# Six places for raw blocks in the y phases, and four small moves around them

## The chip, the cores and the metric

The kernel runs on one core of a Trainium2 chip. A core has five engines that run side by side, each with its own queue of instructions: PE (matrix products, 128 x 128 weights against up to 512 columns), DVE (vector work), ACT (copies and activations), POOL (here only small powers and products) and SP (here only the issue of transfers between the device memory and the on-chip memory). Engines wait for one another by semaphores. The metric is the device time of one execution in microseconds (us).

## The reference

Two kinds of layers are applied in turn, each twice, to a 2048 x 512 matrix `x`, all in float32:

```python
def _A_ref(x, dft_seq_re, dft_seq_im, dft_hid_re, dft_hid_im):
    a = jnp.einsum("bsd,ed->bse", x, dft_hid_re)
    b = jnp.einsum("bsd,ed->bse", x, dft_hid_im)
    y = jnp.einsum("ts,bse->bte", dft_seq_re, a) - jnp.einsum("ts,bse->bte", dft_seq_im, b)
    return y

def _B_ref(x, w1, w2, w3, w4):
    h = _gelu(_layernorm(x, axis=-1) @ w1)
    # the four quarters of h are shifted by +1, -1, +2, -2 rows
    hs = jnp.concatenate([g0, g1, g2, g3], axis=-1) @ w2
    x1 = x + hs
    h2 = _gelu(_layernorm(x1, axis=-1) @ w3) @ w4
    return x1 + h2

x = x + _A_ref(_layernorm(x, axis=-1), ...)
x = x + _B_ref(_layernorm(x, axis=-1), B_w1, B_w2, B_w3, B_w4)
x = x + _A_ref(_layernorm(x, axis=-1), ...)
x = x + _B_ref(_layernorm(x, axis=-1), B_w1, B_w2, B_w3, B_w4)
```

## The kernel before, in words

**Products.** Each float32 operand is split into a high part (rounded to the type `fp32r`) and a low part (the rest). A product is three matmuls (`mm3`, lines 282 to 284): high by high, high by low, low by high. So every block that comes from memory goes through ACT (the high part, a cast) and DVE (the low part, a subtraction) before PE may use it.

**Layer A.** The 2048 rows of the result are made in four chunks `c` of 512. The sequence transform is done with the block tricks of a fast matrix product, so that a chunk has two phases of eight steps `k`: an x phase (`x_phase`, products of sums of the input blocks in `ax`) and a y phase (`y_phase`, products of the blocks in `ay`). The hook of an x phase counts half steps, `i` from 0 to 15. Chunk 0 of the first layer is done without these sums (`plain_phase`), while the input is normed for the first time. A y phase has for each `k` two items, `by1` and `by0`, of 12 matmuls each, 192 in all. An item's block is the difference of two blocks of the transform matrix: DVE makes the difference (line 234, `ring..f<-raw,raw`), ACT its high part (line 235), DVE its low part (line 245). The hidden transform of chunk `c` (`hid`, tiles `rr`) runs inside the x phase of chunk `c + 1`; that of the last chunk runs behind the last y phase.

**The queue of blocks.** `pieces` lists all blocks in the order of their loading, 512 KB each, `items` the split blocks in the order of their use. A raw block lands in one of four places (`raw_at`, piece `i` in place `i % 4`), is split into one of four slots of `ring`, and PE reads the slots. `issue_dma` writes the next load into SP's program as soon as all items that use the place's old block stand in the program. SP issues in that order, and an issue waits until the old block has in fact been read. SP's one queue also carries the stores and loads of the rows of the result (`rows`: `x1d`, `xs`, `tmp`) and the shuffles `zd`, `zt`. The program keeps eight completion counters in turn, so that a transfer's issue also waits for the transfer eight ahead of it.

**Around the last y phase of a layer.** The result of a chunk is added to the input (`add_y`) in two halves of two tiles, followed by their row statistics (`y_stats`: DVE, then two operations of POOL) and a store to `x1d`. For chunk 2 the first half comes in the x phase of chunk 3, and the statistics of the second half (tiles 10 and 11) run at `k == 2` of the y phase of chunk 3 (`late["y"]`). In the same stretch the first four tiles are prepared for layer B: they are loaded back into `xs` (`BACK`), normed on ACT (line 330; tiles 0 and 1 at half step 12 of the x phase, 2 and 3 at half step 15), transposed by four DVE operations at `k == 0` of the y phase (line 594, `turned`), stored in shuffled order (`zd`, four transfers) and loaded again (`zt`).

**Layer B.** Behind the last hidden transform comes the mix (`by_pairs`): 32 slots, `shifted` (product with `w1`, gelu, shift) and `mixed` (product with `w2`), four of each for a chunk. The lists `D(slot, ...)` and `A(slot, ...)` hang other work on slots: `D` ahead of the slot's own DVE or ACT work, `A` behind it. Then the pairs of chunks go through the two large products; the last pair ends the program.

**The head.** Before the first matmul the first tile of the input is summed up by `stats` (DVE and POOL), DVE writes the first normed quarter blocks (`part_highs`, line 327), ACT the high part of the first half block (line 1465), DVE its low part (`block_low`, line 1468). The first matmuls stand in line 414: four of high by high, four of high by low, four of low by high, and again for the second pair of banks.

Of the kernel before, what the change touches and what calls it, by code (L numbers as in the profile page):

```python
# [43 lines left out]
def spectral_mlp_kernel(ctx: ExitStack, tc: tile.TileContext, x, ws, hs, w1, w2, w34, out):  # L44
# [58 lines left out]
    rg = [[at(f"rg{i}{g}", RR + (4 * i + g) * 2 * CH, 2, CH) for g in range(KD)] for i in range(2)]  # L103
    ring, ringf = zip(*(both(f"ring{i}", RNG + i * 4 * CH, 2, 2, CH) for i in range(RING)))
    raw_at = [at(f"raw{i}", RAWS + i * 2 * CH, 2, CH, dtype=F32) for i in range(RAW)]

    blk, blkf = {}, {}
    for i, word in (("11", H3), ("21", H3 + 4 * CH), ("12", RNG), ("22", RNG + 4 * CH)):
# [34 lines left out]
        return tmps[(count["tmp"] - 1) % len(tmps)]  # L143


    pieces, items, w_items, w_pieces = [], [], [], []

    def piece(src, a=0, b=2):
        pieces.append((src, a, b))
# [10 lines left out]
    for layer in range(LAYERS):  # L160
        for c in range(NC):
            if layer == 0 and c == 0:
                for k in range(NP):
                    item("plain", piece(ws[c, k][:, 2:4]))
                    item("plain", piece(ws[c, k][:, 0:2]))
                continue
            for k in range(NP):
                if c:
                    for h in range(NP):
                        if HAT[h] == k:  # L170
                            item("plain", piece(hs[HORDER[h % 4]]))
                p = piece(ws[c, k][:, 2:4])
                item("plain", p)
                item("one", p, span=(0, 1))
            ps = [(piece(ws[c, k][:, 2:4]), piece(ws[c, k][:, 0:2])) for k in range(NP)]
            for k, kind in y_order():
                item(kind, *ps[k])
        for o in HORDER:
            item("plain", piece(hs[o]))
        w_items.append(len(items))  # L180
        for i in range(2):
            item("plain", piece(w1[i]), dest=w12[i])
        for i in range(2):
            item("plain", piece(w2[i]), dest=w12[2 + i])
        w_pieces.append(len(pieces))
# [5 lines left out]
    state = {"dma": 0, "one": 0, "two": 0, "use": 0, "made": 0, "done": 0, "limit": 0, "load": w_pieces[0]}  # L191
    x_left = [(0, 1), (1, 1)] + [(j, 2) for j in range(2, NT, 2)]

    def load_x():
# [8 lines left out]
    def issue_dma(upto=None):  # L203
        while state["dma"] < (state["load"] if upto is None else upto):
            i = state["dma"]
            if i >= RAW and any(n >= state[stage] for n, stage in uses[i - RAW]):
                break
            src, a, b = pieces[i]
            raws[i] = raw_at[i % RAW]
            nc.sync.dma_start(raws[i][:, a:b], src)  # L210
            state["dma"] += 1
            if i % 2 and i > 3:
                load_x()
# [261 lines left out]
    def x_phase(c, hook):  # L475
        h = 0
        for k in range(NP):
            first, last = k == 0, k == NP - 1
            while c and h < NP and HAT[h] == k:
                s = stream()  # L480
                ri, dp = HORDER[h % 4]
                hid(ri, dp, s, PD, 2 * (h // 4), h % 4 == 0, h % 4 == 3)
                if h % 4 == 3:
                    add_y(c - 1, h // 4, PD, X1, 2 * k if h < 4 else "y")
                h += 1
            s = stream()
            run_late(2 * k)
# [75 lines left out]

    ln1, ln2 = {}, {}

    def add_y(c, half, ps, to, defer=None):
        j = c * TC + 2 * half
        for i in range(2):
            add(to[:, i], ps[i], to[:, i])
        if defer is None:  # L570
            y_stats(j, to)
        else:
            late.setdefault(defer, []).append(lambda: y_stats(j, to))

    def y_stats(j, to):
        for known, mrs in zip((ln1, ln2), stats_twice([to[:, 0], to[:, 1]])):
# [137 lines left out]
    def by_pairs(layer, zs, xin, dst):  # L714
# [17 lines left out]
        def A(slot, *fs):  # L732
            todo.setdefault((slot, 1), []).extend(fs)
# [115 lines left out]
        A(4, z_highs(1))  # L849
        D(5, z_lows(1))  # L850

        A(1, back(10, x1d), norm(8, 9))
        D(2, turn(sc0, 2, 0))
        D(3, turn(sc0, 2, 1))
        A(5, norm(10, 11))
# [588 lines left out]
    for layer in range(LAYERS):  # L1444
# [4 lines left out]
        for c in range(NC):  # L1449
            if layer == 0 and c == 0:  # L1450
                raws[0] = raw_at[0]
                for i in (1, 0):
                    load_x()
                    nc.sync.dma_start(raws[0][:, i], pieces[0][0][:, i])
# [35 lines left out]

                xp[0] = stats([xt(0)])
                block_high(1)
                block_low(1)
                part_highs(0)
                normed_act(pairs[0][:, 0], xt(0), xp[0][0])
                block_high(0)
                xp[0] += stats([xt(1)])
# [41 lines left out]
            def hook(i):  # L1539
                k, odd = divmod(i, 2)  # L1540
                if layer == 0 and c == 1:
# [4 lines left out]
                    if i == 3:  # L1546
                        xp_lows(NP - 1, False)
                    w4_split(2 * NP + i)
                if c == 0:
                    if layer:  # L1550
                        for step, f in zip((0, 0, 1), (ay_sums, ay_highs, ay_lows)):
# [29 lines left out]
            def hook(k):  # L1581
# [15 lines left out]

        tmps[:] = singles
        count["tmp"] = 0
# [2 lines left out]
        for i, (ri, dp) in enumerate(HORDER):  # L1602
# [76 lines left out]
```

## Time and profile before

| | |
|---|---|
| median of 3 runs | 1429.75 us (1428.42 to 1429.76) |
| the profiled execution | 1429.24 us, its span 1427.3 us |
| PE busy | 1420.0 us, 6261 instructions |
| DVE busy | 1168.8 us |
| ACT busy | 732.1 us |
| POOL busy | 79.7 us |
| transfers | 307.57 MB, 215 GB/s over the span |

The span goes from the first instruction's start to the last one's end. Matmuls overlap, so the busy time of PE says nothing of small gaps: those are read from the distance between the starts of matmuls. "idle before" is the time that an engine stood still ahead of an instruction, and behind `<-` stands what ended it. An SP row tells when a transfer was issued; where rows are merged (`x4`), the time is that of all of them.

### The profile page before, as it was taken

How to read it: one execution, taken by the hardware profiler on the slowest of the kernel's cores; microseconds unless marked ns; L12 is line 12 of the kernel's file. 1: busy time of each engine (PE TensorE's matmuls, PEld its weight loads, DVE VectorE, ACT ScalarE, POOL GpSimd, SP SyncE). 2: the span in 40 equal slices, each digit the busy share in tenths (PEclk: the TensorE clock that was granted, in tenths of full speed). 3: DMA queues.
4: the chain of work that ended last, by engine and by line, in shares of the span. 5: the costliest groups of instructions: out<-in, count | busy, mean ns of one | idle time of the engine just before them, and what ended most of it. 6: DMA issues, size and time to landing. Idle time of an engine off the chain costs nothing.

```text
span 1427.3 us, 17317 instructions
## 1 busy us (share of the span) xinstructions
PE 1420.0 (99%) x6261; PEld 1173.8 (82%) x6261; DVE 1168.8 (82%) x1642; ACT 732.1 (51%) x992; POOL 79.7 (6%) x105
## 2 busy tenths in 40 slices
PE   9999999999999999999999999999999999999998
PEld 7888888888888888888888888888877888888887
DVE  7986998988979888666799989889889787656676
ACT  5663464455565754434455644544555665433351
POOL 2100000000002000000000000000000020000000
PEclk9999999999999999999999999999999999999999
DMA  7866656657754857944645566575777458477764
GB/s 253 278 207 206 206 191 223 212 175 270 270 163 121 290 199 253 362 159 164 223 160 191 182 231 211 175 244 184 232 250 240 139 156 309 159 243 282 241 206 159
DMA packets 127828, 307.57 MB, mean 215 GB/s; under 512 B 9216, under 2 KB 50176, under 8 KB 124544
## 3 DMA queue, kind: packets, MB, share of 16 engines
q1 hardware_dynamic: 127744, 306.48, 64.2%
q8 instruction: 49, 0.80, 0.2%
q14 instruction: 35, 0.29, 0.1%
HBM read 252.18 MB, written 54.26 MB: 215 GB/s over the span
## 4 chain that ended last, share of the span: by engine, by line
PE 96%; DVE 2%; DMA 2%; issue 0%; SPq 0%; ACT 0%; DVEq 0%
PE psd L283 10%; PE psd L282 10%; PE psd L284 10%; PE psa L283 8%; PE psa L282 8%; PE psa L284 8%; PE psc L283 7%; PE psc L284 7%; PE psc L282 7%; PE psb L283 7%; PE psb L282 7%; PE psb L284 7%; DMA raw<-in_ws 2%; DVE ring L245 1%; DVE ring2f L234 0%
## 5 line engine op out<-in xcount | busy, mean ns | idle before, releaser
L228 ACT CAST ring<-raw 128x1024 fp32r<-128x1024 f32 x127 | 132.9, 1052 | 80.3 <-PE psd L284 41.1
L245 DVE TENSOR_TENSOR ring<-raw,ring 128x1024 fp32r<-128x1024 f32 x126 | 153.4, 1219 | 12.8 <-ACT ring L228 12.6
L282 PE MATMUL psd<-ring,rr 128*128 128x512 f32 x208 | 80.9, 389 | 0.0
L283 PE MATMUL psd<-ring,rr 128*128 128x512 f32 x208 | 80.9, 389 | 0.0
L284 PE MATMUL psd<-ring,rr 128*128 128x512 f32 x208 | 80.9, 389 | 0.0
L322 POOL TENSOR_TENSOR rs<-ve,mhalf 128x4 f32<-128x4 f32 x16 | 28.7, 1796 | 609.6 <-DVE nm L321 609.6
L301 POOL TENSOR_TENSOR rs<-ve,mhalf 128x2 f32<-128x2 f32 (+2 forms) x33 | 28.8, 872 | 547.5 <-DVE nb L300 528.6
L235 ACT CAST ring<-ring0f 128x1024 fp32r<-128x1024 f32 x28 | 29.5, 1054 | 57.7 <-DVE ring0f L234 57.7
L619 ACT ACTIVATE tmp<-rest 128x512 f32<-128x512 f32 x30 | 19.0, 632 | 73.2 <-DVE rest L468 72.8
L245 DVE TENSOR_TENSOR ring<-ring1f,ring 128x512 fp32r<-128x512 f32 (+1 forms) x56 | 53.2, 950 | 0.7 <-ACT ring L231 0.7
L330 ACT ACTIVATE tmp<-xs,nb,rs 128x512 f32<-128x512 f32 x56 | 43.2, 808 | 14.4 <-POOL nb L302 13.1
L283 PE MATMUL psb<-ring,ay 128*128 128x512 f32 x128 | 50.2, 392 | 0.4 <-DVE ring L245 0.4
L283 PE MATMUL psc<-ring,ay 128*128 128x512 f32 x128 | 49.9, 390 | 0.3 <-DVE ring L245 0.3
L282 PE MATMUL psb<-ring,ay 128*128 128x512 f32 x128 | 49.8, 389 | 0.0
L284 PE MATMUL psb<-ring,ay 128*128 128x512 f32 x128 | 49.8, 389 | 0.0
L284 PE MATMUL psc<-ring,ay 128*128 128x512 f32 x128 | 49.8, 389 | 0.0
L282 PE MATMUL psc<-ring,ay 128*128 128x512 f32 x128 | 49.8, 389 | 0.0
L235 ACT CAST ring<-ring1f 128x1024 fp32r<-128x1024 f32 x28 | 29.5, 1054 | 39.2 <-DVE ring1f L234 39.2
L282 PE MATMUL psa<-ring,ay 128*128 128x512 f32 x126 | 49.2, 390 | 0.3 <-ACT rr00f L501 0.3
L283 PE MATMUL psa<-ring,ay 128*128 128x512 f32 x126 | 49.1, 389 | 0.0
L282 PE MATMUL psd<-ring,ay 128*128 128x512 f32 x126 | 49.0, 389 | 0.0
L283 PE MATMUL psd<-ring,ay 128*128 128x512 f32 x126 | 49.0, 389 | 0.0
(657 smaller groups left out, 4439.9 us busy)
## 6 DMA issues: line engine op xcount, KB each, us to landing
raw<-in_ws SPq DMA_DIRECT2D x183, 512.0 KB, 5.0
w4r<-w4d SPq DMA_DIRECT2D x66, 512.0 KB, 4.4
raw<-in_hs SPq DMA_DIRECT2D x56, 512.0 KB, 3.6
w3b<-w3d SPq DMA_DIRECT2D x14, 1792.0 KB, 7.9
w3d<-w3b SPq DMA_DIRECT2D x5, 1792.0 KB, 6.9
x1d<-tmp SPq DMA_DIRECT2D x12, 512.0 KB, 6.2
xs<-x1d SPq DMA_DIRECT2D x12, 512.0 KB, 5.2
w4d<-w4in SPq DMA_DIRECT2D x11, 512.0 KB, 5.0
```

The source lines that it names most:

```text
L228: nc.scalar.copy(dest[:, a:b, 0], r[0][:, a:b])
L235: nc.scalar.copy(dest[:, :, 0], lo)
L245: nc.vector.tensor_tensor(lo, src, hi.bitcast(F32), op=ALU.subtract)
L282: nc.tensor.matmul(o, lh, rh, start=first, stop=False, skip_group_check=more)
L283: nc.tensor.matmul(o, lh, rl, start=False, stop=False, skip_group_check=more)
L284: nc.tensor.matmul(o, ll, rh, start=False, stop=last, skip_group_check=more)
L301: nc.gpsimd.tensor_tensor(rs[:, :n], ve[:, :n], mhalf[:, 0, :n], op=ALU.pow)
L322: nc.gpsimd.tensor_tensor(rs, ve, mhalf[:, :, :2], op=ALU.pow)
L330: nc.scalar.activation(o, s, AF.Identity, bias=mr[2], scale=mr[1])
L619: nc.scalar.activation(g_of, ps_of, AF.Gelu_apprx_tanh)
```

## The change

Five edits, all in the order of work; no arithmetic is changed.

1. Two more places for raw blocks are laid over parts of the on-chip memory that are free in the y phases (one over a buffer of the `w4` weights' preparation). They are open from half step 11 of an x phase to the end of the y phase behind it (`state["wide"]`), for the blocks of y phases alone. A load now takes the free place whose block is oldest, not place `i % 4`. This holds for all seven y phases.
2. In the y phase of chunk 3 the norms of tiles 2 and 3 move from half step 15 of the x phase to `k == 0` of the y phase, and the four transposes are split: two at `k == 0`, two at `k == 1`.
3. The statistics of tiles 10 and 11 leave this y phase: they run in slot 2 of the mix, on the copy of the rows that is loaded into `xs[5]`.
4. That load moves ahead, from slot 1 of the mix into the hidden transform ahead of it.
5. In the head, `part_highs(0)` stands ahead of `block_low(1)`.

The names behind an underscore in the rows below are buffer numbers; `raw4` and `raw5` are the new places, and line numbers of the changed program are up to 11 higher.

DVE at the start of the program, before and then changed: `rr00` and `ay0` are the first normed quarter blocks, `ring0<-raw0` is the low part of the first half block.

```order
L299 TENSOR_SCALAR ve_294<-mv_290 128x1
L300 TENSOR_SCALAR nb_292<-mv_290 128x1
L1468 TENSOR_TENSOR ring0_176<-raw0_184,ring0_176 128x512
L327 TENSOR_SCALAR rr00_160<-xs0_149,mv_290,rs_291 128x256
L327 TENSOR_SCALAR ay0_108<-xs0_149,mv_290,rs_291 128x256
L296 BN_STATS st_310<-xs0_149 128x6
```

```order
L310 TENSOR_SCALAR ve_296<-mv_292 128x1
L311 TENSOR_SCALAR nb_294<-mv_292 128x1
L338 TENSOR_SCALAR rr00_160<-xs0_149,mv_292,rs_293 128x256
L338 TENSOR_SCALAR ay0_108<-xs0_149,mv_292,rs_293 128x256
L1479 TENSOR_TENSOR ring0_176<-raw0_184,ring0_176 128x512
L307 BN_STATS st_312<-xs0_149 128x6
```

The two normed blocks pass the low part; what follows is the same.

DVE in the y phase of chunk 3 of the second layer, before and then changed, from the items of `k == 1` on (`ring..f<-raw,raw` is the difference for one item, `ring<-ring..f` the low part of the item ahead):

```order
L245 TENSOR_TENSOR ring2_180<-ring2f_181,ring2_180 128x2x512
L594 STREAM_TRANSPOSE turned0_157<-tmp_68 128x16x32 x4
L234 TENSOR_TENSOR ring0f_177<-raw1_185,raw0_184 128x2x512
L245 TENSOR_TENSOR ring3_182<-ring3f_183,ring3_182 128x2x512
...
L245 TENSOR_TENSOR ring2_180<-ring2f_181,ring2_180 128x2x512
L316 BN_STATS st_7614<-tmp_68 128x6 x2
L318 BN_AGGR mv_7611<-st_7614 128x2 x2
L319 TENSOR_SCALAR ve_7615<-mv_7611 128x2
L320 TENSOR_SCALAR ve_7615<-mv_7611 128x2
L321 TENSOR_SCALAR nm_7616<-mv_7611 128x2
L234 TENSOR_TENSOR ring0f_177<-raw1_185,raw0_184 128x2x512
```

```order
L256 TENSOR_TENSOR ring2_180<-ring2f_181,ring2_180 128x2x512
L603 STREAM_TRANSPOSE turned0_157<-tmp_68 128x16x32 x2
L245 TENSOR_TENSOR ring0f_177<-raw0_184,raw3_187 128x2x512
L256 TENSOR_TENSOR ring3_182<-ring3f_183,ring3_182 128x2x512
L245 TENSOR_TENSOR ring1f_179<-raw0_184,raw3_187 128x2x512
L256 TENSOR_TENSOR ring0_176<-ring0f_177,ring0_176 128x2x512
L603 STREAM_TRANSPOSE turned0_157<-tmp_68 128x16x32 x2
L245 TENSOR_TENSOR ring2f_181<-raw2_186,raw1_185 128x2x512
```

Two transposes stand one pair of items later, and the seven instructions of the statistics are gone from this place.

SP in the same stretch, before and then changed: `raw<-in_ws` loads a block, `x1d` takes finished rows, `zd1` the transposed tiles.

```order
L201 DMA xs1_150<-x1d_76 128x2x512
L210 DMA raw2_186<-in_ws 128x1024
L210 DMA raw3_187<-in_ws 128x1024
L201 DMA xs2_151<-x1d_76 128x2x512
...
L201 DMA x1d_76<-tmp_68 128x2x512
L210 DMA raw2_186<-in_ws 128x1024
L210 DMA raw3_187<-in_ws 128x1024
L604 DMA zd1_78<-turned0_157 32x16x128 x4
L210 DMA raw0_184<-in_ws 128x1024
L210 DMA raw1_185<-in_ws 128x1024
```

```order
L204 DMA xs1_150<-x1d_76 128x2x512
L221 DMA raw5_189<-in_ws 128x1024
L221 DMA raw4_188<-in_ws 128x1024
L221 DMA raw3_187<-in_ws 128x1024
L221 DMA raw0_184<-in_ws 128x1024
L204 DMA xs2_151<-x1d_76 128x2x512
...
L221 DMA raw2_186<-in_ws 128x1024
L613 DMA zd1_78<-turned0_157 32x16x128 x4
L221 DMA raw5_189<-in_ws 128x1024
L221 DMA raw4_188<-in_ws 128x1024
```

One pair of loads more stands ahead of `xs2` and ahead of the four `zd1` stores; behind those only one pair of y blocks is left, where there were two.

The diff, without the unchanged lines:

```diff
@@ places and state
+    raw_at += [at(f"raw{RAW + i}", word, 2, CH, dtype=F32) for i, word in enumerate((EXT + 4 * D, STG))]
...
+            y_pieces.update(i for p in ps for i in p)
...
+    held = {i: None for i in range(len(raw_at))}
@@ def issue_dma(upto=None):
             i = state["dma"]
-            if i >= RAW and any(n >= state[stage] for n, stage in uses[i - RAW]):
+            free = [
+                r
+                for r, p in held.items()
+                if (r < RAW or state["wide"] and i in y_pieces)
+                and (p is None or all(n < state[stage] for n, stage in uses[p]))
+            ]
+            if not free:
                 break
             src, a, b = pieces[i]
-            raws[i] = raw_at[i % RAW]
+            r = min(free, key=lambda r: (-1 if held[r] is None else held[r], r))
+            held[r] = i
+            raws[i] = raw_at[r]
@@ def x_phase(c, hook):
-                    add_y(c - 1, h // 4, PD, X1, 2 * k if h < 4 else "y")
+                    at_mix = c == NC - 1 and h > 4
+                    add_y(c - 1, h // 4, PD, X1, "10" if at_mix else 2 * k if h < 4 else "y", xs[5] if at_mix else X1)
@@ def add_y
-        late.setdefault(defer, []).append(lambda: y_stats(j, to))
+        late.setdefault(defer, []).append(lambda: y_stats(j, to if kept is None else kept))
@@ def by_pairs
-        A(1, back(10, x1d), norm(8, 9))
+        A(1, norm(8, 9))
+        D(2, lambda: run_late("10"))
         D(2, turn(sc0, 2, 0))
@@ the head
                 block_high(1)
+                part_highs(0)
                 block_low(1)
-                part_highs(0)
@@ x phase, hook
+                if i == 11:
+                    state["wide"] = True
...
-                if c == NC - 1 and i in (12, 15):
-                    for j in (0, 1) if i == 12 else (2, 3):
+                if c == NC - 1 and i == 12:
+                    for j in (0, 1):
                         normed_act(tmp[:, j], xt(j), ln2[j])
@@ y phase, hook
-                if c == NC - 1 and k == 0:
-                    for q in range(TC):
+                if c == NC - 1 and k < 2:
+                    for q in (2 * k, 2 * k + 1):
                         turn_one(turned0, q, tmp[:, q])
+                    for j in (2, 3)[: 2 - 2 * k]:
+                        normed_act(tmp[:, j], xt(j), ln2[j])
...
             y_phase(c, hook)
+            state["wide"] = False
@@ the last hidden transform
-            if i < 2:
-                j = (6, 8)[i]
+            if i < 3:
+                j = (6, 8, 10)[i]
                 rows(xs[j // 2], x1d, j, 2, True)
```

More of the change, by code (lines that the diff above doesn't have):

```diff
@@ L143, in tmp_tile @@
         return tmps[(count["tmp"] - 1) % len(tmps)]
-    pieces, items, w_items, w_pieces = [], [], [], []
+    pieces, items, w_items, w_pieces, y_pieces = [], [], [], [], set()
     def piece(src, a=0, b=2):
@@ L190, in spectral_mlp_kernel @@
     raws, slots, sums = {}, {}, {}
-    state = {"dma": 0, "one": 0, "two": 0, "use": 0, "made": 0, "done": 0, "limit": 0, "load": w_pieces[0]}
+    held = {i: None for i in range(len(raw_at))}
+    state = {"wide": False, "dma": 0, "one": 0, "two": 0, "use": 0, "made": 0, "done": 0, "limit": 0, "load": w_pieces[0]}
     x_left = [(0, 1), (1, 1)] + [(j, 2) for j in range(2, NT, 2)]
@@ L564, in spectral_mlp_kernel, with add_y @@
     ln1, ln2 = {}, {}
-    def add_y(c, half, ps, to, defer=None):
+    def add_y(c, half, ps, to, defer, kept=None):
         j = c * TC + 2 * half
@@ L569, in add_y @@
             add(to[:, i], ps[i], to[:, i])
-        if defer is None:
-            y_stats(j, to)
-        else:
-            late.setdefault(defer, []).append(lambda: y_stats(j, to))
+        late.setdefault(defer, []).append(lambda: y_stats(j, to if kept is None else kept))
     def y_stats(j, to):
@@ L1451, in spectral_mlp_kernel @@
                 raws[0] = raw_at[0]
+                held[0] = 0
                 for i in (1, 0):
```

## The prediction

> **What bounds the kernel.** I read the head of the page first, then who PE waited for, then the starts of its matmuls phase by phase, and at the one phase that is too long the chain of work and the rows of the other engines.
>
> ```profile
> span 1427.3 us, 17317 instructions
> PE 1420.0 (99%) x6261; PEld 1173.8 (82%) x6261; DVE 1168.8 (82%) x1642; ACT 732.1 (51%) x992; POOL 79.7 (6%) x105
> ```
>
> ```profile
> PE psd L137 <- POOL mhalf L56: 1.4, 1, 1.4
> PE psb L414 <- DVE rr L327: 1.1, 1, 1.1
> PE psb L283 <- DVE ring L245: 0.4, 1, 0.4
> PE psc L283 <- DVE ring L245: 0.3, 1, 0.3
> PE psa L282 <- ACT rr00f L501: 0.3, 1, 0.3
> ```
>
> PE is the bound. Its waits (total us, times, longest) are 1.1 at the first real matmul and three short ones. The view of stretches (start:end, length, then the busy time of PE, PEld, DVE, ACT, POOL, the granted clock, the DMA share) gives three y phases, cut at the starts of their first matmul and of the next phase's first one: chunk 3 of the first layer, chunk 2 and chunk 3 of the second.
>
> ```profile
> 344.17:387.85 43.68, 43.68 (x194) 35.96 (x192) 42.62 (x47) 22.43 (x26) 2.23 (x2) 1.00 0.73 248
> 951.51:995.03 43.52, 43.52 (x193) 36.04 (x192) 40.31 (x43) 20.99 (x25) 2.23 (x2) 1.00 0.60 200
> 1049.43:1095.21 45.78, 44.73 (x194) 35.68 (x193) 43.52 (x47) 22.39 (x26) 2.24 (x2) 1.00 0.71 233
> ```
>
> A y phase has 192 matmuls. The middle one takes 43.52, so one matmul per 0.2267 us at a granted clock of 1.00. Chunk 3 takes 0.16 more in the first layer and 2.26 more in the second. With 1.1 at the head, that is about all a reordering can win: 3.5 us of 1429, or 0.25%. Anything beyond must come as a loss.
>
> The Trainium skill ("TensorE: Matmul & The Clock Gate", "Wait — 56ns, not 53.3ns?") puts warm matmuls at N / 2.4 GHz + about 2.5 ns from start to start, an estimate of 215.8 ns for 512 columns and 41.4 us for this phase; by it the long phase would hold 4.4 us and the sum below would be 2.1 larger. The three rows here agree on 226.7 at different DMA shares, and I go by them.
>
> **Edits 2 and 3, the last y phase of a layer.** First what stops PE there. Of ACT, DVE and PE in the second layer:
>
> ```profile
> 1051.94 1.52 ACT L330 ACTIVATE tmp<-xs,nb,rs 128x512 f32<-128x512 f32 x2
> 1053.36 1.04 ACT L501 COPY rr00f<-psa 128x512 f32<-128x512 f32 x2
> ```
>
> ```profile
> 1054.22 2.49 DVE L594 STREAM_TRANSPOSE turned<-tmp 128x512 f32<-128x512 f32 x4
> 1056.62 1.19 DVE L234 TENSOR_TENSOR ring0f<-raw,raw 128x1024 f32<-128x1024 f32 x1
> 1057.72 1.22 DVE L245 TENSOR_TENSOR ring<-ring3f,ring 128x1024 fp32r<-128x1024 f32 x1
> ```
>
> ```profile
> 1061.63 0.39 PE L282 MATMUL psc<-ring,ay 128*128 128x512 f32 x1
> ```
>
> The two norms (1.52) stand on ACT ahead of the drain of `psa`, which PE waits for; the four transposes (2.49) hold the low part of `ring3` until 1058.94. Item `by1` of `k` = 2, the fifth, starts at 1061.63; without stops it would at 1049.43 + 4 x 12 x 0.2267 = 1060.31. So 1.32 of the 2.26 is lost by then, the other 0.94 later.
>
> With the norms behind the drain, `psa` is free 1.5 earlier, against a wait of 0.3. The norms then stand ahead of the cast of `ring0`, whose source DVE writes no earlier than now; that is their cover, and if it went they would cost their 1.52 less the slack of a ring slot. With two transposes instead of four DVE reaches the low part of `ring3` 1.2 earlier, at 1057.7, and PE needs it one matmul into the fourth item, 1049.43 + 3 x 2.72 + 0.23 = 1057.8. So this is just enough even if no block lands earlier; the later two transposes have DVE's lead behind them, 2.72 - 2.2 (two operations, 1.1 from start to start) = 0.5 per item.
>
> The statistics cost DVE the distance between two rows:
>
> ```profile
> 1065.67 1.28 DVE L316 BATCH_NORM_STATS2 st<-tmp 128x6 f32<-128x512 f32 x2
> 1067.42 1.23 DVE L234 TENSOR_TENSOR ring0f<-raw,raw 128x1024 f32<-128x1024 f32 x1
> ```
>
> 1.75 us. DVE is then left with 43.52 - 1.75 = 41.8 of work in a phase of 43.52. The first layer's phase shows that it can do 42.62 in 43.68 with PE losing 0.16, so 41.8 fits. In the mix the same 1.75 lands in slot 2, in front of a transpose:
>
> ```profile
> 1124.65 0.71 DVE L594 STREAM_TRANSPOSE scr<-extra 128x512 f32<-128x512 f32 x1
> 1126.65 0.69 DVE L659 TENSOR_TENSOR rg<-gt,rg 128x512 fp32r<-128x512 f32 x1 [1.29 <-ACT rg L658]
> ```
>
> ```profile
> 1127.88 0.39 PE L282 MATMUL psd<-w,rg 128*128 128x512 f32 x1
> 1129.69 0.39 PE L284 MATMUL psd<-w,rg 128*128 128x512 f32 x1
> ```
>
> DVE idles 1.29 between these two rows, so the low part of `rg` ends 0.5 later, near 1127.8; PE reads it in the ninth matmul of the slot, at 1129.69. Cost nothing, with 1.9 of cover in each layer. POOL's power and product follow the statistics to where POOL is idle; the norm that needs them hangs on slot 5, three slots on. The load of `xs[5]` (edit 4) only moves ahead, behind the weights; nothing there waits for it.
>
> **Edit 1, the places.** The later 0.94 is late blocks. From the chain of work (start, us), from DVE, and from SP:
>
> ```profile
> 1043.93 5.62 DMA raw<-in_ws
> ...
> 1065.03 7.81 DMA raw<-in_ws
> ...
> 1076.86 5.02 DMA raw<-in_ws
> ```
>
> ```profile
> 1082.01 1.22 DVE L234 TENSOR_TENSOR ring1f<-raw,raw 128x1024 f32<-128x1024 f32 x1 [1.00 <-DMA raw<-in_ws]
> ```
>
> ```profile
> 1065.49 5.34 SPq L604 DMA_DIRECT2D zd<-turned  x4
> 1070.95 6.34 SPq L210 DMA_DIRECT2D raw<-in_ws  x4
> ```
>
> A block takes 5 to 8 us from issue to landing, and with four places a pair is asked for only when the pair two ahead has been read: two pairs are 2 x 24 x 0.2267 = 10.9 us of PE, less DVE's own lead. With six there are 16.3. The blocks that arrive last (landed near 1076.86 + 5.02 = 1081.9) were asked for behind four `zd` stores that held SP 5.34. In the new order one pair more stands ahead of these stores, and the last pair may be issued some 5 us later than it must. A raw load moved past `x1d` delays that store by two issues; its buffer is overwritten at the phase's end, far behind. So I take all 0.94. In the other five y phases nothing waits now (the 43.52 row is one of them), so the places can only cost there: two more loads in flight, nothing as long as no other transfer is needed sooner. For the extra traffic the trace has no row; the bounds are nothing and, if each of the seven phases lost what the busier first-layer phase loses, 7 x 0.16 = 1.1; I take nothing, since that loss has the four transposes beside it. A gain there is excluded by 43.52 being PE's own pace.
>
> The DMA page of the Trainium skill ("DMA: Bandwidth & Descriptors", "Queues, rings and completion order") says that each DMA engine takes descriptors in ring order, so transfers behind the extra raw blocks wait for them. The long landings above agree; by this rule alone `zd` would land later by two blocks, and it is a reason for the third rival below.
>
> **Edit 5, the head.**
>
> ```profile
> 4.98 0.62 ACT L1465 CAST ring<-raw 128x512 fp32r<-128x512 f32 x1 [2.75 <-DMA raw<-in_ws]
> ```
>
> ```profile
> 8.05 0.73 POOL L301 TENSOR_TENSOR rs<-ve,mhalf 128x1 f32<-128x1 f32 x1 [2.59 <-DVE nb L300]
> ```
>
> ```profile
> 5.63 0.69 DVE L1468 TENSOR_TENSOR ring<-raw,ring 128x512 fp32r<-128x512 f32 x1 [1.08 <-ACT ring L1465]
> 6.24 0.41 DVE L327 TENSOR_SCALAR rr<-xs,mv,rs 128x256 fp32r<-128x256 f32 x1
> ...
> 7.96 0.41 DVE L1489 TENSOR_TENSOR rr<-tmp,rr 128x256 fp32r<-128x256 f32 x1
> ...
> 8.83 0.41 DVE L327 TENSOR_SCALAR rr<-xs,mv,rs 128x256 fp32r<-128x256 f32 x1
> ```
>
> ```profile
> 6.79 0.70 PE L414 MATMUL psb<-ring,rr 128*128 128x512 f32 x2 [1.05 <-DVE rr L327]
> ...
> 8.71 0.61 PE L414 MATMUL psb<-ring,rr 128*128 128x512 f32 x2
> ```
>
> DVE stands still until 5.63 for ACT's cast. The normed blocks need only POOL's power, which for this tile took 0.56:
>
> ```profile
> 4.64 0.56 POOL L301 TENSOR_TENSOR rs<-ve,mhalf 128x1 f32<-128x1 f32 x1 [3.28 <-DVE nb L300]
> ```
>
> It ends at 5.20; at the second tile DVE started 0.05 behind the power (8.05 + 0.73 to 8.83), so `rr` runs from 5.25 to 5.66 and the first matmul, 0.14 behind it as now (6.65 to 6.79), starts at 5.80: 0.99 sooner. But DVE's chain begins only 5.63 - 5.25 = 0.38 sooner and holds the same work. The low part of `rr` ends at 7.96 + 0.41 - 0.38 = 7.99, PE may take it at 8.13, and it does so at 8.71 now: 0.58 is left. One more point is tight, in step `k` = 1:
>
> ```profile
> 17.28 0.69 DVE L357 TENSOR_TENSOR rr<-tmp,rr 128x512 fp32r<-128x512 f32 x1 [2.29 <-ACT rr L351]
> ```
>
> ```profile
> 18.23 0.39 PE L284 MATMUL psb<-ring,rr 128*128 128x512 f32 x1
> ```
>
> Ready at 17.97 + 0.14 = 18.11, used at 18.23. Shifted by the same 0.38 it is ready at 17.73; so PE gains 0.50 there. Between 0.38 (DVE's shift alone) and 0.99 I take 0.50, since the tight row comes last.
>
> **The sum.** 0.50 + 2.26 + 0.16 = 2.92 us. Against the profiled execution, 1429.24 - 2.92 = 1426.3 (its span 1424.4, the rest as before). The median shown is 0.5 above that execution: against it the ratio is 0.9976, against the execution itself 0.9980. So the likeliest value lies close to the bound of 0.2% (2.9 us), which is about what a measurement of this kernel can tell from no change; 1426.9 is that bound from the median.
>
> **Rivals.**
>
> *Half of the y phase stays.* The blocks still come late behind `zd`, or DVE, at 41.8 of 43.52, ends last in their place. Then 0.94 stays: 1426.3 + 0.94 = 1427.3, and with nothing at the head 1427.8. For it: DVE is busy all but 1.7 us. Against it: in the first layer's phase it is as busy and PE loses 0.16. This is also the case in which the places do nothing.
>
> *More at the head.* If the normed blocks' chain is not what PE meets next, 0.99: 1425.8. Against it stand the two rows above.
>
> *Slower: SP stands at the `zd` stores.* Three of the four would now find a raw load eight ahead of them still in flight and wait, with the last pair queued behind. They hold SP 5.34 now, from 1065.49, and in the new program SP comes to them no later. PE needs the last pair from item 14 on, at 1049.43 + 13 x 2.72 = 1084.8; less a landing of 8 and 2.3 for DVE's two operations it must be issued by 1074.5. So up to 9 us at the stores costs nothing, and each us above costs one, in two phases. To lose over 0.2% the stores must give back the gain too: 9 + 2.9 = 11.9, which gives 1426.3 + 2 x 2.9 = 1432.1. It is the only queue I see in which the change can lose more than it wins; that all four have their predecessors issued together, and so landed together, speaks against it.
>
> *A faster pace.* If 0.2267 were itself a slowdown by traffic, fewer stops could shorten it. The three phases at DMA shares from 0.60 to 0.73 bound that at nothing, so it gives the time of the sum or a little below; 0.01. The page on TensorE is what speaks for it.
>
> **Chances.** The sum as worked out 0.56, half of the y phase 0.26, more at the head 0.09, slower 0.08, the pace 0.01. The sum's value is 0.6 under the bound and runs scatter over 1.3 (1428.42 to 1429.76), its own range 1425.7 to 1427.0, so of 0.56 I count 0.45 as faster and 0.11 as the same. Faster 0.45 + 0.09 + 0.01 = 0.55; the same 0.11 + 0.26 = 0.37; slower 0.08. The range goes from 1425.8 less 0.5 of scatter to 1427.8 plus 0.7: 1425.3 to 1428.5; it leaves out the slower case and some edges.
>
> **What would show it.** Right: the first matmul of line 414 near 5.8 and a second wait of some 0.4 at the low part of `rr`; the last y phase of both layers at 43.5; no wait of PE on `ring` there; the idle time of DVE on raw blocks gone; `rg` in slot 4 as punctual as now. Wrong: a y phase above 44, a wait at `rg` in the mix, SP rows of `zd` over 9 us, or one of the other five y phases above 43.52.

## The result and the profile after

The changed kernel takes 1426.45 us (median of 10, 1425.84 to 1426.82); the kernel before, beside it, 1429.76 (10 runs, 1428.42 to 1431.24). The ratio is 0.998 (0.9977 worked out from the medians), its 95% interval 0.9971 to 0.9988: 3.3 us less, and 1.7 at the least by that interval. A second comparison, described below, gave 1426.34 against 1428.97, 0.9984 (0.9975 to 0.9993). So the gain is real and lies about at the bound of 0.2%, on both sides of it. The runs of the changed kernel spread over 1.0 us, those of the kernel before over 2.8 here and over 3.6, 4.1 and 2.4 in three larger sets. In the experiments below the spread goes with late blocks, as the gain does.

The profiled execution took 1426.34 us. From the head of its page, and then who PE waited for:

```profile
span 1424.3 us, 17304 instructions
PE 1419.1 (100%) x6261; PEld 1174.5 (82%) x6261; DVE 1169.2 (82%) x1642; ACT 734.4 (52%) x992; POOL 77.7 (5%) x105
```

```profile
PE psd L138 <- POOL mhalf L56: 1.4, 1, 1.4
```

Of the five waits that this view had before, only the start of the program is left; two shorter stops, 0.30 in the head and 0.21 at 739.00, show only in the starts of matmuls. The view of stretches, cut at the same three y phases as in the prediction (columns as there):

```profile
343.91:387.43 43.52, 43.52 (x194) 36.05 (x192) 42.74 (x41) 24.46 (x29) 0.00 (x0) 1.00 0.74 245
951.06:994.58 43.52, 43.52 (x193) 36.04 (x192) 41.11 (x44) 22.63 (x27) 2.23 (x2) 1.00 0.58 185
1048.98:1092.50 43.52, 43.52 (x193) 36.04 (x192) 42.74 (x41) 24.46 (x29) 0.00 (x0) 1.00 0.73 245
```

All three stand at PE's own pace. Between the two profiled executions the last y phase of layer 2 gives 2.26, that of layer 1 0.16, and everything ahead of the first y phase 0.26 (its first matmul starts at 148.07, before at 148.33). The other 0.3 of the 3.0 in the span lies nearly all behind the last y phase of layer 2, and I did not follow it.

SP at the `zd` stores and at the raw blocks around them (start, us, what, number):

```profile
1062.80 0.80 SPq L221 DMA_DIRECT2D raw<-in_ws  x2
1063.65 3.99 SPq L613 DMA_DIRECT2D zd<-turned  x4
1068.06 2.72 SPq L221 DMA_DIRECT2D raw<-in_ws  x2
```

The stores hold SP 3.99 (5.34 before; in layer 1 it is the other way, 4.15 for 2.72), and the last pair of blocks is asked for at 1068.06, 19.1 into the phase (before at 1076.49, 27.1 into it). In the mix, DVE and then PE:

```profile
1121.81 1.28 DVE L327 BATCH_NORM_STATS2 st<-xs 128x6 f32<-128x512 f32 x2
...
1124.18 0.65 DVE L668 TENSOR_TENSOR rg<-gt,rg 128x512 fp32r<-128x512 f32 x1
```

```profile
1126.95 0.39 PE L295 MATMUL psd<-w,rg 128*128 128x512 f32 x1
```

With the statistics in front, the low part of `rg` ends at 1124.83 and PE reads it at 1126.95, so 2.1 of cover is left. It stands 0.2 later than before against its phase, where 0.5 was expected.

### The profile page after: what moved, and what is told of

Read it like the earlier page. It is cut to its first block, busy times and chain, and to the rows that moved or that the text cites. A ratio compares the mean times of both kernels' runs of the same rounds, so it can differ in the third digit from the quotient of the medians.

```text
span 1424.3 us, 17304 instructions
## 1 busy us (share of the span) xinstructions
PE 1419.1 (100%) x6261; PEld 1174.5 (82%) x6261; DVE 1169.2 (82%) x1642; ACT 734.4 (52%) x992; POOL 77.7 (5%) x105
## 4 chain that ended last, share of the span: by engine, by line
PE 95%; DVE 2%; ACT 1%; issue 1%; POOL 0%; DMA 0%; DVEq 0%; POOLq 0%; ACTq 0%
PE psd L294 9%; PE psd L295 9%; PE psd L293 9%; PE psa L294 8%; PE psa L295 8%; PE psa L293 8%; PE psc L294 7%; PE psc L295 7%; PE psc L293 7%; PE psb L294 7%; PE psb L295 7%; PE psb L293 7%; DVE ring L256 0%; DVE xs L970 0%; DVE ay L406 0%
## 5 line engine op out<-in xcount | busy, mean ns | idle before, releaser
L293 PE MATMUL psa<-ring,ay 128*128 128x512 f32 x126 | 49.0, 389 | 0.0
L294 PE MATMUL psa<-ring,ay 128*128 128x512 f32 x126 | 49.0, 389 | 0.0
L295 PE MATMUL psa<-ring,ay 128*128 128x512 f32 x126 | 49.0, 389 | 0.0
```

Source lines behind the costliest of these rows:

```text
L293: nc.tensor.matmul(o, lh, rh, start=first, stop=False, skip_group_check=more)
L294: nc.tensor.matmul(o, lh, rl, start=False, stop=False, skip_group_check=more)
L295: nc.tensor.matmul(o, ll, rh, start=False, stop=last, skip_group_check=more)
```

## The experiments

Each is the changed kernel with something undone or added. Times are medians of 10 or 11 runs with their range; "to before" is the difference to the kernel before in the same comparison (medians 1428.76, 1429.02 and 1428.97), with 95% intervals near 1.3 us either way, most of which is the scatter of the kernel before. The last two columns are the length of the last y phase of each layer in the profiled execution (43.52 is PE's pace).

| kernel | time, us | to before | layer 1 | layer 2 |
|---|---|---|---|---|
| places_only | 1426.69 (1426.36 to 1427.97) | -2.1 | 43.55 | 43.55 |
| no_places | 1428.70 (1427.24 to 1429.55) | -0.1 | 44.49 | 43.56 |
| norms_early | 1426.42 (1426.20 to 1426.90) | -2.3 | 43.52 | 44.15 |
| stats_in_y | 1426.49 (1426.23 to 1426.91) | -2.3 | 43.52 | 43.52 |
| five_places | 1426.49 (1426.24 to 1426.73) | -2.5 | 43.52 | 43.52 |
| wide_late | 1426.91 (1426.01 to 1428.35) | -2.1 | 44.39 | 44.63 |
| zd_late | 1427.29 (1426.73 to 1428.43) | -1.7 | 44.35 | 44.21 |
| no_zd | 1427.24 (1426.35 to 1428.59) | -1.7 | 43.89 | 44.29 |
| zd_twice | 1430.10 (1428.78 to 1433.71) | +1.1 | 45.19 | 44.89 |
| old_head | 1426.53 (1426.27 to 1426.78) | -2.5 | 43.52 | 43.51 |
| after_again | 1426.34 (1426.05 to 1426.88) | -2.6 | 43.52 | 43.52 |
| best | 1430.64 (1430.52 to 1431.43) | +1.7 | 43.52 | 43.52 |

### Which part makes the gain

**places_only**: the places stay, the rest goes back (but for edit 4, which moves one load).

```
-                if c == NC - 1 and i == 12:
-                    for j in (0, 1):
+                if c == NC - 1 and i in (12, 15):
+                    for j in (0, 1) if i == 12 else (2, 3):
...
-                if c == NC - 1 and k < 2:
-                    for q in (2 * k, 2 * k + 1):
+                if c == NC - 1 and k == 0:
+                    for q in range(TC):
...
-                    add_y(c - 1, h // 4, PD, X1, "10" if at_mix else 2 * k if h < 4 else "y", xs[5] if at_mix else X1)
+                    add_y(c - 1, h // 4, PD, X1, 2 * k if h < 4 else "y")
...
-                part_highs(0)
                 block_low(1)
+                part_highs(0)
```

> The places stay; the four transposes together, the early norms, the statistics in the y phase and the old order of the head come back. Theory A (the prediction's split: norms and transposes cost 1.32 of the 2.26, late blocks 0.94): the last y phase of layer 2 takes 43.52 + 1.32 = 44.8, PE stops at psa and at the low part of ring3 and not later; time 1426.4 + 1.32 + 0.16 + 0.3 (head) = 1428.2. Theory B (the extra blocks, asked for before the phase starts, take away the 1.38 that DVE idled just ahead of it, and with that both early stops): 43.5 to 43.7, time 1426.8. Theory C (places do nothing): 45.8, 1429.7.

**no_places**: four places only; the rule that takes the free place with the oldest block stays.

```
-                if i == 11:
-                    state["wide"] = True
```

> The changed kernel with four places only. Theory A: late blocks cost 0.94 again: last y phase of layer 2 44.5, time 1427.4, with PE's stop near 35 us into the phase and none before. Theory B: DVE's idle time of some 1.4 ahead of the phase is back, the lighter start of the phase just covers it, so nothing early; late blocks 0 to 0.9. Theory C (DVE's load alone made the stops): 43.52, 1426.4.

**norms_early** undoes edit 2 alone (the first two hunks of places_only).

> The changed kernel with both pairs of norms in the x phase and the four transposes together at the start of the y phase, as before. Theory A: 1.32 comes back: last y phase of layer 2 44.8, of layer 1 43.5 to 43.7, time 1427.7. Theory B: the places have DVE and ACT ahead by then: at most 0.2, time 1426.4 to 1426.7.

**stats_in_y** undoes edit 3 alone (the `add_y` line of places_only).

> The changed kernel with the statistics of the last pair in the y phase again (1.75 us of DVE). Theories A and B: DVE has 43.5 of work in 43.52, but is ahead at the start: 0 to 0.2 in each layer, time 1426.4 to 1426.8. Theory D (DVE's load decides the second half of the phase): 0.9 or more, 44.4 and 1427.3.

In places_only theory B holds: with the places alone the two phases are within 0.03 of PE's pace (43.55 and 43.55). Without them nothing of the gain is left (1428.70 against 1428.76). None of the three theories gave that time: theory A had the place of the stop right, 25 to 34 us into layer 1's phase and none early, but not the size, and theory B expected DVE to stand idle for 1.4 ahead of the phase, where this execution shows 0.33 in layer 2 and nothing in layer 1. The execution profiled (1427.31) is the second fastest of the ten, so no trace shows where the other 1.4 of the median go. Where the early part went is seen on DVE just ahead of the last y phase of layer 2. Before:

```profile
1047.07 1.22 DVE L245 TENSOR_TENSOR ring<-ring0f,ring 128x1024 fp32r<-128x1024 f32 x1
1049.67 1.22 DVE L234 TENSOR_TENSOR ring2f<-raw,raw 128x1024 f32<-128x1024 f32 x1 [1.38 <-PE psa L284]
```

And places_only, with the same norms, transposes and statistics:

```profile
1047.08 1.22 DVE L256 TENSOR_TENSOR ring<-ring0f,ring 128x1024 fp32r<-128x1024 f32 x1
1048.28 1.22 DVE L245 TENSOR_TENSOR ring2f<-raw,raw 128x1024 f32<-128x1024 f32 x1
```

The row of before puts DVE's 1.38 down to PE. But `ring2` takes the block that the chain of waits shows from 1043.93 on with 5.62, so until 1049.55, 0.12 ahead of the start. DVE entered the phase 1.39 late because of a block, and behind the four transposes that became PE's stop some 10 us on. With SP's rows of places_only one sees why the block is there in time:

```profile
1036.33 7.93 SPq L221 DMA_DIRECT2D raw<-in_ws  x4
```

Four blocks are asked for here between 1036 and 1044; before, it was two:

```profile
1037.89 6.37 SPq L210 DMA_DIRECT2D raw<-in_ws  x2
```

What a late entry costs depends on the order of work behind it. I call DVE late by as much as this first difference (`ring2f`) starts later against the phase than in the changed kernel. In the executions profiled, with norms and transposes in the old order, PE has lost by its fifth item nearly what DVE was late: 1.3 of 1.39 (before, layer 2), 1.1 of 1.15 and 0.9 of 0.91 (wide_late, layers 2 and 1), 0.6 of 0.71 (norms_early, layer 2) and 0.1 of 0.22 (before, layer 1). In the order of edit 2 a lateness of 1.02 (zd_late, layer 2) cost nothing by then, and one of 1.76 (no_zd, layer 2) cost 0.5. These kernels follow below; the two rows:

```profile
1049.39 1.23 DVE L245 TENSOR_TENSOR ring2f<-raw,raw 128x1024 f32<-128x1024 f32 x1 [1.00 <-DMA raw<-in_ws]
```

```profile
1050.58 1.23 DVE L245 TENSOR_TENSOR ring2f<-raw,raw 128x1024 f32<-128x1024 f32 x1 [1.74 <-DMA raw<-in_ws]
```

So the early stops need both, a late block and the old order. The places make the late block rare, and edit 2 lets DVE be about 1.0 late at no cost.

The statistics are worth nothing that shows: in stats_in_y DVE is busy 43.41 of 43.52 in both phases, and PE loses nothing: with six places DVE starts 1.2 ahead of the phase and may use the whole of it. Edits 2 and 3 together leave the median nearly where it was (1426.69 to 1426.53, old_head) but cut the spread: five of the ten runs of places_only are above 1426.8, none of old_head's is.

norms_early shows how little a single execution says. Its profiled execution, the slowest of its ten, lost 0.63 at the low part of `ring3`, because DVE was 0.71 late there although four blocks had been asked for as early as in places_only; its median is that of the changed kernel. no_places lost 0.97 in layer 1 and next to nothing in layer 2, the kernel before 0.16 and 2.26. Which phase loses, and how much, changes from execution to execution.

### How many places, and from when

**five_places**: one place more than before.

```
-    raw_at += [at(f"raw{RAW + i}", word, 2, CH, dtype=F32) for i, word in enumerate((EXT + 4 * D, STG))]
+    raw_at += [at(f"raw{RAW + i}", word, 2, CH, dtype=F32) for i, word in enumerate((EXT + 4 * D,))]
```

> The changed kernel with one place more than before instead of two. Blocks are used in pairs, so theory P2 (a pair must be in flight more): one more place lets only one block of the pair go early and the other is asked for as late as before: 1427.5 or more. Theory L (each block asked for earlier helps; what is missing is less than one block, 1.3 to 2.3 us): 1426.4 to 1426.7.

**wide_late**: norms_early, and the places open at the start of the y phase.

```
-                if i == 11:
-                    state["wide"] = True
...
+            state["wide"] = True
             y_phase(c, hook)
```

> norms_early (1426.4) with the places opened only when the y phase starts, not in the x phase's last items. Theory B1 (the early stops go because two blocks are asked for before the phase starts): DVE's idle time of about 1.4 just ahead of the last y phase is back, and with the early norms and four transposes together PE stops at psa and ring3 again, 1.3 in layer 2: 1427.4 to 1427.8. Theory B2 (the places matter only against the lateness behind zd): 1426.4 to 1426.7.

Beside the other edits one more place does it all (1426.49, spread 0.5), as theory L forecast: each block that is asked for earlier helps, and it need not be a pair. wide_late lies between its theories in the median, 0.5 above norms_early, and its spread is 2.3 against 0.7. Its profiled execution, the slowest of its ten, has the early stops again. From DVE ahead of the phase, and from who PE waited for:

```profile
1049.87 1.23 DVE L245 TENSOR_TENSOR ring2f<-raw,raw 128x1024 f32<-128x1024 f32 x1 [1.13 <-DMA raw<-in_ws]
```

```profile
PE psb L294 <- DVE ring L256: 0.8, 2, 0.4
```

Here the row names the DMA. So the blocks asked for ahead of the phase matter (B1), though not in every execution.

### What makes the blocks late

**zd_late**: no_places, with the stores three items later.

```
-                if c == NC - 1 and k == 2:
+                if c == NC - 1 and k == 5:
                     turn_out(turned0)
```

> Four places as in no_places (1428.7), but the four zd stores three items later (at k = 5 instead of 2), behind most of the phase's raw blocks. Theory Z (blocks land late because the zd stores, which move little data at a high DMA share, take the DMA engines from them): no stop of PE 20 to 35 us into the last y phases, time 1426.4 to 1427.0. Theory P (four places are too few in any case: a block of 5 to 8 us from issue to landing against two pairs of PE's work): stops stay, 1428.0 to 1429.0.

**no_zd**: no_places without them.

```
-                    turn_out(turned0)
+                    count["turn"] += 1
...
+                if c == 1 and k == 2:
+                    z = zd[(count["turn"] + 1) % 2].rearrange("(d p) t -> p d t", p=P)
+                    nc.sync.dma_start(z, ay[0].bitcast(F32).rearrange("p a b c -> p a (b c)"))
```

> Four places (no_places, 1428.7) without the four zd stores in the y phase (left out, so the transposed block that the mix reads is not the right one; another store fills that memory two chunks earlier). Theory Z (the stores' share of the DMA engines makes the blocks late): no stop, 1426.4 to 1426.6. Theory P (four places are too few in any case): stops of some 0.8 per layer as in zd_late, 1427.0 to 1427.5, DVE still waiting for blocks in the phase.

**zd_twice**: the changed kernel with the stores made twice.

```
                 if c == NC - 1 and k == 2:
                     turn_out(turned0)
+                    turn_out(turned0, zcopy)
```

> The changed kernel with the four zd stores made twice (the second time to memory that nothing reads). The third rival of the prediction (SP held at the stores; free up to 9 us, from there each us costs one): SP is held 8 to 9 instead of 4.0, time 1426.4 to 1427.0. If the stores' traffic makes the blocks late (theory Z), twice the stores use up what the two places won: 1427.5 to 1429.

Both causes are at work. With four places, moving or removing the stores gives back 1.4 in the medians (1428.70 to 1427.29 and 1427.24), or 1.7 if each is taken against the kernel before beside it, of the 2.3 to 2.6 that the changed kernel gains. The rest stays even with no such store (0.35 of it, in no_zd's execution, lies in chunk 1 of layer 2, where the store that replaces them stands). no_zd lies in the range of theory P, zd_late between the two theories. The view of DMA issues around the stores of layer 1 (raw blocks, size, median us from issue to landing) of no_places and of no_zd:

```profile
raw<-in_ws SPq DMA_DIRECT2D x6, 512.0 KB, 6.4
```

```profile
raw<-in_ws SPq DMA_DIRECT2D x6, 512.0 KB, 5.6
```

A block lands 0.8 later beside the stores (over the whole last y phase 5.8 against 5.1 in layer 1 and 5.3 against 4.9 in layer 2), and without them it is still too late for four places in some executions.

zd_twice is the prediction's third rival made real, and its 1430.10 lies above both forecasts. SP in its layer 1:

```profile
358.74 4.02 SPq L614 DMA_DIRECT2D zd<-turned  x4
362.81 5.37 SPq L614 DMA_DIRECT2D zcopy<-turned  x4
368.27 2.08 SPq L222 DMA_DIRECT2D raw<-in_ws  x2
```

Then DVE and PE:

```profile
376.05 1.22 DVE L246 TENSOR_TENSOR ring1f<-raw,raw 128x1024 f32<-128x1024 f32 x1 [4.24 <-DMA raw<-in_ws]
377.19 1.22 DVE L257 TENSOR_TENSOR ring<-ring0f,ring 128x1024 fp32r<-128x1024 f32 x1
```

```profile
376.72 0.39 PE L294 MATMUL psc<-ring,ay 128*128 128x512 f32 x1
378.46 0.50 PE L295 MATMUL psc<-ring,ay 128*128 128x512 f32 x1 [1.36 <-DVE ring L257]
```

SP is held 9.5 and the phase loses 1.67. DVE waits 4.24 for the last pair, and behind that wait stands the low part of `ring0`, which PE needs one item earlier. It is SP's hold that makes the pair late and not a slower landing: the two blocks take 6.2 from issue to landing here, and 6.5 in the changed kernel. Layer 2 shows the same: held 8.8, 1.37 lost, landing in 6.3 and in 6.4.

### The head

**old_head** undoes edit 5 alone (the last hunk of places_only).

> The changed kernel with the head's old order. By the prediction 0.50 comes back: 1426.9. By the two profiles 0.27, of which 0.2 hangs on when the first x tile lands: 1426.7. If the head's gain is used up by the first stop behind it: 1426.4. First matmul of line 425 at 6.8 instead of 6.0 in each case.

**after_again** and **best**: the changed kernel once more, and with two edits that were meant to gain further.

```
-                    for _, t, h in parts[i]:
-                        normed(t[:, 0], xt(i)[:, h * DH : (h + 1) * DH], xp[0][i])
+                    for f, (_, t, h) in zip((normed, normed_act), parts[i]):
+                        f(t[:, 0], xt(i)[:, h * DH : (h + 1) * DH], xp[0][i])
...
-X6, X7 = 2, 4
+X6, X7 = 2, 5
```

> The changed kernel once more, so that it stands beside best on one chip: 1426.4 to 1426.5, all y phases 43.52.

> The changed kernel with two more edits. In the head ACT makes the normed blocks of ay (DVE has 0.33 less per tile), so the low part of rr should end 0.33 earlier and the second stop (0.29, with 0.11 on the matmul behind it) go: y phases start 0.3 to 0.4 sooner. In the x phase of layer 2's first chunk the statistics of the eighth pair come one item later (X7 = 5), which takes 1.6 of DVE's work from in front of the ring slot that PE waits for at 739.0: 0.32 sooner. Both: 1425.7. If the first is given back in step k = 1: 1426.0; if the second stop only moves to a later item: 1426.1; if neither is worth anything: 1426.4.

The old order costs 0.1 in the median, within the spread of either. In the profiles it shows better: the first y phase starts at 148.31 to 148.46 in the three executions with the old order, and at 147.76 to 148.34, 148.10 on average, in ten with the new one (without best), so 0.26 sooner. PE in the changed kernel's profile:

```profile
1.36 4.57 PE L138 MATMUL psd<-ident 128*128 128x128 f32 x24 [1.36 <-POOL mhalf L56]
...
6.00 0.70 PE L425 MATMUL psb<-ring,rr 128*128 128x512 f32 x2
...
7.48 0.61 PE L425 MATMUL psa<-ring,ay 128*128 128x512 f32 x2
8.23 0.74 PE L425 MATMUL psb<-ring,rr 128*128 128x512 f32 x2
```

and DVE:

```profile
3.59 0.69 DVE L307 BATCH_NORM_STATS2 st<-xs 128x6 f32<-128x512 f32 x1 [3.59 <-DMA xs<-in_x]
...
5.44 0.41 DVE L338 TENSOR_SCALAR rr<-xs,mv,rs 128x256 fp32r<-128x256 f32 x1 [0.69 <-POOL rs L312]
...
7.76 0.41 DVE L1500 TENSOR_TENSOR rr<-tmp,rr 128x256 fp32r<-128x256 f32 x1
...
17.09 0.69 DVE L368 TENSOR_TENSOR rr<-tmp,rr 128x512 fp32r<-128x512 f32 x1 [2.30 <-ACT rr L362]
```

In this execution the first tile of x came at 3.59, before at 3.38, and everything on DVE stands those 0.2 later than worked out: the first matmul at 6.00 for 5.80, the low part of `rr` done at 8.17 for 7.99. best was to take 1425.7 and takes 1430.64. Its second stop in the head shrinks from 0.30 to 0.11, but the tight step `k` = 1 takes that back: PE loses 0.5 there in four late starts, and the first y phase starts at 148.23. So that step bounds the head next.

best's other edit cost 4 us at one place. DVE and PE in the x phase of layer 2's first chunk:

```profile
735.76 0.69 DVE L256 TENSOR_TENSOR ring<-ring3f,ring 128x512 fp32r<-128x512 f32 x1 [2.16 <-ACT ring L242]
...
737.30 1.28 DVE L307 BATCH_NORM_STATS2 st<-xs 128x6 f32<-128x512 f32 x2
...
740.79 0.68 DVE L256 TENSOR_TENSOR ring<-ring1f,ring 128x512 fp32r<-128x512 f32 x1
```

```profile
740.92 0.50 PE L294 MATMUL psc<-ring,ax 128*128 128x512 f32 x1 [1.79 <-DVE ring L256]
741.26 0.40 PE L295 MATMUL psc<-ring,ax 128*128 128x512 f32 x1
...
743.18 0.63 PE L295 MATMUL psb<-ring,ax 128*128 128x512 f32 x1
743.61 0.63 PE L293 MATMUL psb<-ring,ax 128*128 128x512 f32 x1
```

In the changed kernel the statistics fill most of the time in which DVE waits for ACT here (0.40 is left there of the 2.16); one item later they stand in front of a slot that PE needs. The x phase takes 36.98 instead of 32.98: the stop of 1.79 was followed by seven matmuls at 0.43 from start to start, and a stop of 0.4 at the end of the phase adds the rest. No kernel here beats the changed one by more than the spread; five_places and stats_in_y equal it with less.

## Why the prediction was right, and where not

**The sum.** 1426.3 was worked out, 1426.45 and 1426.34 measured, and the three phases end at 43.52 as put down. The total is right; three of its terms are not what they were said to be.

**1.32 by the norms and transposes: half of the cause.** The step that failed is the reading of the early stops. I took the rows between 1051.94 and 1058.94 as the cause because they stand ahead of PE's stop, and did not ask why DVE began 1.39 late. That edit 2 is enough without an earlier block was nearly right: in its order 1.02 late cost nothing and 1.76 late 0.5. But norms_early (1426.42) and places_only show that the places take these stops away without it, and edit 2 without places does nothing for the median (no_places has it).

**0.94 by late blocks: right in kind, too small.** The places are worth 2.1 to 2.5, all of the y phases' gain. The cover that I gave them (ahead of the `zd` stores, the last pair with time to spare) is as in SP's rows above. That the blocks are late behind the `zd` stores is some two thirds of it, 1.4 to 1.7 by zd_late and no_zd.

**The size of 2.26.** It came from one execution. no_places, with the same cause, spreads over 2.3 us and lost in the other layer. That the sum fits the medians is partly luck: the execution shown lay near the middle of a kernel that runs from 1426.94 to 1431.24.

**Statistics, `xs[5]`, `x1d`: cost nothing, right**, with 2.1 of cover at `rg`. "DVE is left with 41.8 of work" was not: it is busy 42.74, since DVE ahead of PE takes work of the next stage into the phase. Nor was the relief needed: 43.41 is no loss.

**The other five y phases: right.** They stand at 43.52 in the changed kernel's profile, so two more loads in flight cost nothing and the bound of 1.1 was empty. One of them, chunk 0 of layer 2, took 43.57 in after_again, and 43.55 in the kernel before, so it was not quite true that nothing waited there.

**The head: the mechanism right, 0.50 mis-sized.** 0.26 in the profiles, 0.1 in the medians (within the spread). 0.2 of the 0.5 is the later tile of this execution, which the starts above put among the ordinary differences. What I left out: the first matmul can now stand directly behind the warm-up and wait for it (last section), and the matmul behind the second stop starts 0.11 late.

**The rivals.** Half of the y phase staying fell: DVE near its limit is no stop as long as blocks are there. More at the head fell with the tight step in `k` = 1. SP at the stores was the right mechanism with too high a point: 9 us were called free, zd_twice loses 1.67 at 9.5 (358.74 to 368.27) and 1.37 at 8.8, so some 7.5 to 7.9 are. The error is one item: I let PE need the last pair with item 14, but DVE handles items in order, and the low part of item 13 is behind the wait. In zd_twice the pair is asked for 24.2 into the phase (which starts at 344.08) and 1.67 is lost, so it must be issued by 22.5 and not by 25.1; the stores of zd_twice begin 1.1 to 1.4 sooner in the phase than I took, which hides half of the error. The change itself holds SP 3.99 there, 4.15 in layer 1. The rule of ring order that stood behind this rival (the Trainium skill, "DMA: Bandwidth & Descriptors", "Queues, rings and completion order") would have `zd` land later by two blocks; the trace does not settle it: the view of DMA issues has these stores at 7.4 from issue to landing in layer 1 of the changed kernel and at 6.7 before, but in layer 2 at 7.6, and at 8.3 before:

```profile
zd<-turned SPq DMA_DIRECT2D x4, 256.0 KB, 7.6
```

The faster pace fell: the y phases in which PE does not stop take 43.52 in every kernel, at DMA shares from 0.53 to 0.77.

## What to carry to other kernels

When the bound engine stops, follow the late engine back to where it first stood idle; the work just ahead of the stop may be only half of the cause, and a row that names an engine long done may hide a transfer. Where a buffer ring is so tight that a load's landing time decides, the loss wanders between phases and executions: one profile shows the mechanism and not the size, and the spread of the runs is the better sign. One or two more buffers, opened before the phase that needs them, were worth more here than the four moves of work beside them; what the moves added is a smaller spread.

## What the hardware did unexpectedly

A stop of 1.79 us cost almost as much again afterwards. The granted clock of best behind it (stretches as above):

```profile
739.00:741.00 2.00, 0.21 (x2) 0.08 (x1) 2.00 (x5) 1.18 (x2) 1.63 (x2) 1.00 0.00 0
741.00:743.00 2.00, 2.00 (x7) 1.64 (x8) 1.07 (x2) 2.00 (x4) 0.00 (x0) 0.75 0.55 127
743.00:745.50 2.50, 2.50 (x7) 1.94 (x7) 1.93 (x2) 1.39 (x3) 0.00 (x0) 0.52 0.29 115
745.50:748.00 2.50, 2.50 (x13) 2.02 (x12) 2.50 (x6) 1.73 (x3) 0.00 (x0) 1.00 0.69 208
```

A mean of 0.75 over 2.0 us and of 0.52 over 2.5 puts the half rate from about 742.0 to 745.4: it begins 1.1 us after PE has started again and lasts 3.4. Seven matmuls at 0.43 instead of 0.23, and two slowed in part, cost 1.6 us. The stop of 1.36 in zd_twice left the clock at 1.00. Each is a single execution, so whether the length of the stop decides, and where the border lies, stays open. The Trainium skill ("TensorE: Matmul & The Clock Gate", "What's actually happening") has the clock go to half after an idle window of about 3.4 us; the half rate agrees with the 0.43, but here a stop of 1.79 was enough.

The warm-up differs between executions: its 24 matmuls start at 1.36 each time and take 4.28 to 5.49. This is stats_in_y, against 4.57 and 6.00 in the changed kernel's rows above:

```profile
1.36 5.49 PE L138 MATMUL psd<-ident 128*128 128x128 f32 x24 [1.36 <-POOL mhalf L56]
6.50 0.87 PE L425 MATMUL psb<-ring,rr 128*128 128x512 f32 x2
```

With the new order of the head the first real matmul can wait for the warm-up itself, which the three executions with the old order did not meet (6.74 to 6.87 there): 0.5 here, of which some 0.2 is left at the first y phase (148.13 to 148.34 in the four executions with the long warm-up, 147.76 to 148.09 in the six others).

Behind most stops, short ones too, the second matmul starts 0.11 late (740.92 to 741.26 in best's rows, 0.34 instead of 0.23; a stop of 0.09 at 348.32 in wide_late lacks it). Four such stops cost 0.44 beside their length.
